# Hash bits for half of the next batch's head pairs, moved from the matrix engine to GpSimd and VectorE

## The chip, the cores and the metric

The kernel runs on one core of one Trainium2 chip. The metric is the device time of one execution in microseconds (us). Engines are named as in the profile: PE is the matrix engine (TensorE) and PEld its weight loads, DVE is VectorE, ACT is ScalarE, POOL is GpSimd, and SP is the engine whose queue issues most of the DMAs. An engine works through its own instructions in the order in which the program lists them; it runs ahead of the other engines as far as its waits allow.

## What is computed

The reference is a hash-masked attention followed by a gated feed-forward block with a residual, in 4 batches of 8 heads, 768 tokens and a head size of 64:

```
bits    = (q @ proj > 0), (k @ proj > 0)            # proj: 64 x 6
mask    = bucket(q)[:, None] == bucket(k)[None, :]  # equal in all six bits
attn    = softmax(where(mask, q @ k.T / 8, -1e9));  x = attn @ v
ffn     = (gelu(x @ w_gate) * (x @ w_val)) @ w_out  # 512 -> 1536 -> 512
out     = x + sigmoid(x @ w_res) * ffn              # 3072 tokens x 512
```

The six bits of each token become +-0.5 values behind the 64 channels of q or k (the tile `nat`). One matmul over 71 rows then gives score and mask penalty together, and `exp` does the rest.

## The kernel before, in words

**Tiling.** Heads go in pairs `p` = 0 to 15, four pairs to a batch. A pair's q (side 0) and k (side 1) are loaded as `[128, 12, 64]` fp32 tiles (`raw`, line 107). `cast` (lines 208, 210, on POOL) writes them as bf16 into `nat`, of which there are four buffers; pair p+2 uses the buffers of pair p. `bits` (line 282) writes the six hash values beside them, and `turn` (line 308) transposes `nat` into `aug` by a DMA from SP. Thus `cast` and `bits` of a pair must wait until the transposing DMA of the pair two before it has landed.

**Stages.** After the first batch's attention (slots 0 to 35, an order written out by hand) the program alternates. A *gate stage* for batch b, `gate_val`, runs 12 steps `m`: 16 matmuls with `w_gate` and 16 with `w_val` into two PSUM buffers `sp` (line 472), a Gelu on ACT (line 489), and the product `hh` on DVE (line 492), which frees the buffer for the next step's second half. Then an *attention stage* for batch b+1 runs 36 slots, nine to a pair: scores (line 448), `exp` on ACT (line 459), the product with v two slots later (line 421), and among these the matmuls of the output projection of batch b (lines 504 and 518), of which DVE makes an output row (lines 521 and 524). Per head, DVE also clears an accumulator (`opened`, line 388), repeats a preset over it (`repeat`, line 400, after the matmul of line 396) and normalises it (`finish`, lines 372 and 373).

**Order around the change.** `gv(b, m, ...)` appends a piece of work behind step m of gate stage b, `at(s, ...)` behind slot s. These set only the order in each engine's queue. For b = 1 and 2 the next batch's first two pairs (`xs`) and last two (`ys`) are prepared so. `tr` (line 240) transposes a raw tile on DVE in 32 x 32 blocks. `hash_mm` (line 251) multiplies these by `proj` on PE, 16 fp32 matmuls in two passes each for two pairs. `hash_tok` (line 266) transposes the sums back, and `bits` takes the signs in four instructions of 32 partitions. In the first attention stage the result of `hash_tok`, `ht`, is in SBUF; later it is in PSUM. `vals_s` and `vals_a` (lines 338 to 350, POOL) prepare v. For `ys`: `tr` at two late slots and behind m = 3 and 5, `cast` behind 5 and 6, `hash_mm` behind 6, `hash_tok` behind 7, `bits` and `turn` behind 7 to 10.

**Last row.** The very last output row is made in two parts, of 384 and 128 columns, each with its matmuls, two DVE instructions and DMA.

Of the kernel before, what the change touches and what calls it, by code (L numbers as in the profile page):

```python
# [9 lines left out]
FP32 = mybir.dt.float32  # L10
BF16 = mybir.dt.bfloat16
AF = mybir.ActivationFunctionType
ALU = mybir.AluOpType
# [33 lines left out]
def kernel(  # L47
# [23 lines left out]
    HT = 2 * T  # L71
# [10 lines left out]
    const = ctx.enter_context(tc.tile_pool(name="const", bufs=1))  # L82
# [19 lines left out]
    x_tok, x_sb = {}, {}  # L102
# [94 lines left out]
    def nat_of(x):  # L197
        return nat[(2 * x[0] + x[1]) % NN]
# [34 lines left out]
    def acc_done(what):  # L233
        accs[len(accs) - 1 - accs[::-1].index(what)] = None

    def tr(p, side, h0=0, h1=2):
        if (p, side) not in t32:
            t32[p, side] = t32_pool.tile([P, HT, 2, 32], FP32, tag="t32", name="t32")
        sl = slice(h0 * T, h1 * T)
        nc.vector.transpose(t32[p, side][:, sl].rearrange("p c h n -> p (c h n)"),  # L240
                            raw[p, side][:, sl].rearrange("p c d -> p (c d)"))
# [15 lines left out]
    def ht_of(jobs):  # L257
        return jobs[0]

    def hash_tok(jobs, psum=False):  # L260
        n = 32 * len(jobs)
        if psum:
            ht = mm_ps.tile([P, HT, 32], FP32, tag=take(("ht", ht_of(jobs))), name="htp")
        else:
            ht = sm_pool.tile([P, HT, 32], FP32, tag="ht", name="ht")
        nc.vector.transpose(ht[:n].rearrange("p c n -> p (c n)"),
                            hsum[jobs[0]][:n].rearrange("p c n -> p (c n)"))
        give(jobs[0])
        for j, x in enumerate(jobs):
            htok[x] = (ht, j)  # L270
        ht_left[id(ht)] = (len(jobs), ("ht", ht_of(jobs)))

    def bits(p, side, engs=(nc.vector,)):
        x = (p, side)
        ht, j = htok.pop(x)
        n, what = ht_left.pop(id(ht))
        if n > 1:
            ht_left[id(ht)] = (n - 1, what)
        else:
            give(what)  # L280
        for a in range(4):
            engs[a % len(engs)].tensor_scalar(  # L282
                nat_of(x)[32 * a:32 * a + 32, :, D:D + NBITS],
                ht[32 * j:32 * j + 32, :, NBITS * a:NBITS * (a + 1)], 0.0, 0.5,
                op0=ALU.is_gt, op1=ALU.subtract)


# [9 lines left out]
    def bits_one(p, side, hi):  # L297
        hs = hsum.pop((p, side, hi))
        nc.vector.transpose(hs[:, 1].rearrange("p c n -> p (c n)"),
                            hs[:, 0].rearrange("p c n -> p (c n)"))  # L300
        nc.vector.tensor_scalar(nat_of((p, side))[:, hi * T:hi * T + T, D:D + NBITS],
                                hs[:, 1, :, 0:NBITS], 0.0, 0.5, op0=ALU.is_gt, op1=ALU.subtract)
        acc_done(("hs", p, side, hi))

    def turn(p, side):
# [29 lines left out]
    def vals_a(p):  # L335
        vs = rawv[p]
        va = va_pool.tile([P, 2, T, D + 2], BF16, tag="va", name="va")
        nc.gpsimd.tensor_copy(va[:, :, :, 0:D], vs)
        nc.gpsimd.memset(va[:, :, :, D:D + 1], 1.0)
        vaug[p] = va  # L340

    def vals_s(p):
        vs = rawv[p]
        vsum = va_pool.tile([P, 2, D + 2], BF16, tag="vsum", name="vsum")
        v3 = sm_pool.tile([P, 2, 3, D], FP32, tag="v3", name="v3")
        nc.gpsimd.tensor_add(v3, vs[:, :, 0:3, :], vs[:, :, 3:6, :])  # L346
        v1 = sm_pool.tile([P, 2, D], FP32, tag="v1", name="v1")
        nc.gpsimd.tensor_add(v1, v3[:, :, 0, :], v3[:, :, 1, :])
# [149 lines left out]
    def project(b):  # L498
        hh = hidden[b]
        for t in range(T):  # L500
            last = b == B - 1 and t == T - 1
            rps = mm_ps.tile([P, DMODEL], FP32, tag=take(), name="rps")
            for kk in range(KM):
                nc.tensor.matmul(rps, x_sb[b][:, kk, t, :], wr[:, kk, :],  # L504
                                 start=(kk == 0), stop=(kk == KM - 1))
                if kk == KM - 1:
                    th = g_pool.tile([P, DMODEL], FP32, tag="th", name="th")
                    nc.scalar.activation(th, rps, AF.Tanh, scale=0.5)  # L508
                yield
            o = o_pool.tile([P, DMODEL], FP32, tag="o", name="o")  # L510
            for k0, k1 in ((0, 3), (3, 4)) if last else ((0, KM),):
                cs = slice(k0 * P, k1 * P)
                if b < B - 1:
                    fps = mm_ps.tile([P, DMODEL], FP32, tag=take(), name="fps")
                else:
                    fps = sc_ps.tile([P, DMODEL], FP32, tag="sp", name="fps")
                for m in range(KF):
                    nc.tensor.matmul(fps[:, cs], hh[:, m, bass.ts(t, P)], wo[:, m, cs],  # L518
                                     start=(m == 0), stop=(m == KF - 1))
                    yield  # L520
                nc.vector.scalar_tensor_tensor(o[:, cs], th[:, cs], 1.0, fps[:, cs],  # L521
                                               op0=ALU.add, op1=ALU.mult)
                o3 = o[:, cs].rearrange("p (k n) -> p k n", n=P)
                nc.vector.scalar_tensor_tensor(o3, o3, 0.5, x_tok[b][:, k0:k1, t, :],
                                               op0=ALU.mult, op1=ALU.add)
                nc.sync.dma_start(out_t[b, t][:, cs], o[:, cs])

# [35 lines left out]
    def at(s, *pieces):  # L563
        side_work.setdefault(s, []).extend(pieces)
# [4 lines left out]
    def gv(b, m, *pieces):  # L569
        gv_work.setdefault((b, m), []).extend(pieces)  # L570
# [92 lines left out]
    for name in ORDER.split():  # L663
        first.pop(name)()

    def lay(b, m, x):
        gv(b, m, lambda: bits(*x), lambda: turn(*x))

    for b in range(B - 1):
        s0, p0 = b * NSLOT, (b + 1) * HP  # L670
        xs = [(p0 + i, side) for i in range(2) for side in range(2)]
        ys = [(p0 + 2 + i, side) for i in range(2) for side in range(2)]
        if b > 0:
            for j, (x, y) in enumerate(zip(xs, ys)):
                at(s0 + 24 + 2 * j, lambda x=x: tr(*x))
                at(s0 + 25 + 2 * j, lambda x=x: cast(*x, nc.gpsimd))
                if j < 2:
                    at(s0 + 32 + 2 * j, lambda y=y: tr(*y))
                loads(s0 + 2 + 4 * j, (x[0], "qk"[x[1]]))
                loads(s0 + 18 + 3 * j, (y[0], "qk"[y[1]]))  # L680
            gv(b, 0, lambda p0=p0: tokens((p0, p0 + 1), True))
            for m, x in zip((0, 1, 2, 4), xs):
                lay(b, m, x)
            gv(b, 3, lambda y=ys[2]: tr(*y))
            gv(b, 5, lambda y=ys[3]: tr(*y))
            for m, y in zip((5, 5, 6, 6), ys):
                gv(b, m, lambda y=y: cast(*y, nc.gpsimd))
            gv(b, 6, lambda p0=p0: hashed((p0 + 2, p0 + 3)))
            gv(b, 7, lambda p0=p0: tokens((p0 + 2, p0 + 3), True))
            for m, y in zip((7, 8, 9, 10), ys):  # L690
                lay(b, m, y)
        else:
            for m, names in enumerate(BESIDE):
                for name in names.split():
                    gv(b, m, first.pop(name))
    for p in range(HP, NPAIR):
# [8 lines left out]
    def mlp_mm(n):  # L705
        while mlp and n > 0:
            try:
# [3 lines left out]
            except StopIteration:  # L711
                mlp.pop(0)

    gate_val(0, begun)
    mlp.append(project(0))
    for s in range(NSLOT, LAST):
# [60 lines left out]
```

## Time and profile before

| | |
|---|---|
| time, median of 3 runs (lowest, highest) | 346.66 us (346.12, 347.13) |
| profiled execution: time, span | 346.07 us, 344.4 us |
| granted PE clock | 0.998 |
| PE busy | 333.5 us, 97% of the span |
| ACT, DVE, POOL busy | 206.2, 191.7 and 85.6 us |
| gate stage of batch 1, of batch 2 | about 129.8 to 162.5 us, 209.5 to 242 us |
| attention of batch 2, of batch 3 | about 162.5 to 209.5 us, 242 to 289 us |

A timeline line has the start and the length in us, the engine, the source line, the operation with its output and inputs, how often it was merged, and in brackets the idle time before it with what ended it. A line of the groups has source line, engine, operation, shapes and count, then busy us and mean ns of one, then idle time before. The span excludes about 1.7 us that lie around it.

### The profile page before, as it was taken

The page shows a single profiled execution, that of the slowest core. Times are in us where ns is not written, and L with a number is a line of the kernel's source. Part 1 is how long each engine was busy: PE and PEld are TensorE (multiplying, and loading weights), DVE is VectorE, ACT ScalarE, POOL GpSimd, SP SyncE. Part 2 cuts the span into 40 slices and gives each one's busy share as a digit, 9 for nine tenths or more (in the row PEclk, how much of TensorE's full clock was granted, in tenths as well). Part 3 has the DMA queues.
Part 4 walks back from the last instruction along what each step waited for, and adds up shares of the span by engine and source line. Part 5 has one row for each costly group of instructions (what it writes and reads, how often), then busy time and mean ns, then how long its engine had stood idle before and what let it go on. Part 6 is the DMA issues. An engine that isn't in the chain of part 4 may idle for free.

```text
span 344.4 us, 7546 instructions
## 1 busy us (share of the span) xinstructions
PE 333.5 (97%) x3064; PEld 204.3 (59%) x3112; DVE 191.7 (56%) x404; ACT 206.2 (60%) x232; POOL 85.6 (25%) x162
## 2 busy tenths in 40 slices
PE   8998999999999999999999999999999999999994
PEld 4675766555666655655666665656566665566442
DVE  6979737656344856757344784747244444343333
ACT  3888972226999962224999982223999984223110
POOL 3887920317055000260043200242030000000000
PEclk9999999999999999999999999999999999999999
DMA  7959998999976743528366642725430220000022
GB/s 215 376 128 280 146 241 149 181 127 176 189 175 188 210 107 78 101 39 148 82 194 188 227 115 65 131 49 109 75 100 32 55 55 30 33 0 0 32 79 75
DMA packets 71171, 42.90 MB, mean 125 GB/s; under 512 B 49504, under 2 KB 68192, under 8 KB 71136
## 3 DMA queue, kind: packets, MB, share of 16 engines
q1 hardware_dynamic: 64720, 37.17, 44.0%
q0 software_dynamic: 6336, 5.24, 10.2%
q8 instruction: 24, 0.39, 0.5%
q14 instruction: 11, 0.09, 0.1%
q10 hardware_dynamic: 80, 0.00, 0.0%
HBM read 29.36 MB, written 6.29 MB: 104 GB/s over the span
## 4 chain that ended last, share of the span: by engine, by line
PE 90%; DVE 3%; ACT 3%; issue 1%; DMA 1%; SPq 0%; POOL 0%; DVEq 0%; ACTq 0%; POOLq 0%
PE sp L472 34%; PE fps L518 18%; PE sp L448 17%; PE av L421 9%; PE rps L504 6%; PE hs L251 3%; ACT hh L459 2%; DMA ld<-in_k_dram 1%; PE pt L320 1%; PE wps L174 1%; DVE nat L282 1%; PE hs L293 1%; DVE aug L329 1%; ACT gt L489 0%; SPq L308 0%
## 5 line engine op out<-in xcount | busy, mean ns | idle before, releaser
L459 ACT ACTIVATE e<-sp 128x1024 bf16<-128x1024 f32 x108 | 109.0, 1028 | 8.0 <-PE sp L448 2.8
L489 ACT ACTIVATE gt<-sp 128x768 bf16<-128x768 f32 x48 | 38.9, 810 | 92.8 <-PE sp L472 92.8
L448 PE MATMUL sp<-aug,aug 71*128 71x256 bf16 (+1 forms) x384 | 85.8, 325 | 2.0 <-DVE aug L329 1.6
L518 PE MATMUL fps<-wo,hh 128*128 128x512 bf16 (+2 forms) x275 | 74.6, 369 | 1.4
L492 DVE TENSOR_TENSOR hh<-gt,sp 128x768 bf16<-128x768 bf16 x48 | 45.7, 953 | 48.0 <-PE sp L472 43.9
L472 PE MATMUL sp<-x_sb,wv 128*128 128x256 bf16 (+1 forms) x378 | 70.6, 325 | 0.7 <-DVE hh L492 0.4
L472 PE MATMUL sp<-x_sb,wg 128*128 128x256 bf16 (+1 forms) x373 | 70.4, 324 | 0.7
L421 PEld LDWEIGHTS <-e 128*128 128x128 bf16 x864 | 40.2, 97 | 25.1
L472 PEld LDWEIGHTS <-wv 128*128 128x128 bf16 x384 | 37.6, 98 | 25.3 <-issue 0.6
L472 PEld LDWEIGHTS <-wg 128*128 128x128 bf16 x384 | 36.7, 98 | 26.0 <-issue 2.3
L421 PE MATMUL av<-va,e 128*128 128x65 bf16 x864 | 43.4, 193 | 0.0
L518 PEld LDWEIGHTS <-hh 128*128 128x128 bf16 x300 | 27.4, 97 | 22.5
L459 ACT ACTIVATE hh<-sp 128x1024 bf16<-128x1024 f32 x36 | 34.4, 1026 | 5.1 <-PE sp L448 5.0
L521 DVE SCALAR_TENSOR_TENSOR o<-th,fps 128x512 f32<-128x512 f32 (+2 forms) x25 | 16.7, 666 | 36.9 <-PE fps L518 30.0
L448 PEld LDWEIGHTS <-aug 71*128 71x128 bf16 x384 | 29.2, 97 | 13.0 <-issue 2.0
L346 POOL TENSOR_TENSOR v<-ldv 128x384 f32<-128x384 f32 x16 | 16.0, 999 | 64.1 <-DMA ldv<-in_v_dram 64.0
L240 DVE STREAM_TRANSPOSE t<-ld 128x768 f32<-128x768 f32 (+1 forms) x34 | 30.5, 912 | 1.6 <-DMA ld<-in_k_dram 1.4
L400 DVE COPY av<-av 128x390 f32<-128x390 f32 x24 | 13.6, 567 | 29.7 <-PE av L396 29.7
L208 POOL TENSOR_SCALAR nat<-ld 128x768 bf16<-128x768 f32 (+1 forms) x16 | 13.8, 860 | 60.1 <-DMA aug<-nat 55.4
L504 PE MATMUL rps<-wr,x_sb 128*128 128x512 bf16 x90 | 25.6, 378 | 0.3
L508 ACT ACTIVATE th<-rps 128x512 f32<-128x512 f32 x24 | 14.3, 594 | 18.5 <-PE rps L504 18.5
L210 POOL CAST nat<-ld 128x768 bf16<-128x768 f32 (+1 forms) x17 | 13.3, 783 | 39.7 <-DMA aug<-nat 38.8
(64 smaller groups left out, 242.5 us busy)
## 6 DMA issues: line engine op xcount, KB each, us to landing
ldv<-in_v_dram SPq DMA_DIRECT2D x16, 384.0 KB, 5.4
out_dram<-o SPq DMA_DIRECT2D x23, 256.0 KB, 2.0
ld<-in_q_dram SPq DMA_DIRECT2D x15, 384.0 KB, 5.6
ld<-in_k_dram SPq DMA_DIRECT2D x15, 384.0 KB, 5.2
wg<-in_moe_w_gate_dram POOLq DMA_DIRECT2D x4, 384.0 KB, 8.5
wv<-in_moe_w_val_dram POOLq DMA_DIRECT2D x4, 384.0 KB, 9.0
wo<-in_moe_w_out_dram POOLq DMA_DIRECT2D x3, 512.0 KB, 9.4
wr<-in_moe_w_res_dram POOLq DMA_DIRECT2D x1, 512.0 KB, 7.7
```

Source lines behind the costliest of these rows:

```text
L240: nc.vector.transpose(t32[p, side][:, sl].rearrange("p c h n -> p (c h n)"), raw[p, side][:, sl].rearrange("p c d -> p (c d)"))
L346: nc.gpsimd.tensor_add(v3, vs[:, :, 0:3, :], vs[:, :, 3:6, :])
L421: nc.tensor.matmul(av[p, hi][:, qt, :], e[:, off:off + P], va[:, hi, jt, 0:D + 1], start=first, stop=(p >= HP and jt == T - 1), skip_group ...
L448: nc.tensor.matmul(sp[:, off:off + nq * P], ks[0:KA, hi * T + jt, :], qs[0:KA, hi * T + qt0:hi * T + qt0 + nq, :], start=True, stop=True)
L459: nc.scalar.activation(e, sp, AF.Exp, scale=float(ALPHA))
L472: nc.tensor.matmul(sp[:, c0:c1], w[:, kk, bass.ts(m, P)], xs[:, kk, c0:c1], start=(kk == 0), stop=(kk == KM - 1))
L489: nc.scalar.activation(gt, sp[:, 0:S], AF.Gelu)
L492: nc.vector.tensor_mul(hidden[b][:, m, :], gt, ps[1][:, 0:S])
L504: nc.tensor.matmul(rps, x_sb[b][:, kk, t, :], wr[:, kk, :], start=(kk == 0), stop=(kk == KM - 1))
L508: nc.scalar.activation(th, rps, AF.Tanh, scale=0.5)
L518: nc.tensor.matmul(fps[:, cs], hh[:, m, bass.ts(t, P)], wo[:, m, cs], start=(m == 0), stop=(m == KF - 1))
L521: nc.vector.scalar_tensor_tensor(o[:, cs], th[:, cs], 1.0, fps[:, cs], op0=ALU.add, op1=ALU.mult)
```

## The change

For b = 1 and 2 the bits of `ys` no longer use PE. `proj` is read once as a row on all partitions and turned to six rows `prow` of 64 (one DMA, one POOL copy, in the first gate stage). For each of the four tiles in `ys` and each of the six bits, POOL multiplies the raw tile by the row (`part`, 768 elements per partition, into a buffer of the ring `t32` of six), DVE sums each run of 64 (`part_sum`), and after six of these one DVE instruction takes the signs (`bits_sum`) and `turn` follows. The lists PROD and SUMS place the 24 products and sums: numbers below 12 stand behind that gate step, 12 and more behind slot n - 12 of the following attention. The `tr`, `hash_mm`, `hash_tok` and `bits` of `ys` are gone. `bits` and `turn` of `xs` move to steps 0, 0, 3, 5, the casts of `ys` to 2, 5, 10, 11, and `vals_s` and `vals_a` to nine and six slots ahead of their pair (both eight before).

Besides: the SBUF result of `hash_tok` gets 15 rows in place of 12, four used and one left out, three times; the first DVE instruction of an output row writes its product over the PSUM input and the second reads it there; the last row is made in parts of 256, 128 and 128 columns, the last of them in another PSUM pool.

```diff
+    def stripes(ht):
+        n = ht.shape[1]
+        return ht.rearrange("p (a c) n -> p a c n", a=3)[:, :, 0:HT // 3] if n > HT else \
+            ht.rearrange("p (a c) n -> p a c n", a=3)
...
-            ht = sm_pool.tile([P, HT, 32], FP32, tag="ht", name="ht")
+            ht = sm_pool.tile([P, HT + 3, 32], FP32, tag="ht", name="ht")
...
-                nat_of(x)[32 * a:32 * a + 32, :, D:D + NBITS],
-                ht[32 * j:32 * j + 32, :, NBITS * a:NBITS * (a + 1)], 0.0, 0.5,
+                nat_of(x)[32 * a:32 * a + 32, :, D:D + NBITS].rearrange("p (a c) n -> p a c n", a=3),
+                stripes(ht[32 * j:32 * j + 32, :, NBITS * a:NBITS * (a + 1)]), 0.0, 0.5,
...
+    hsum6 = const.tile([P, HT + 3, NBITS], FP32, name="hsum6")
+    prow = const.tile([P, NBITS, D], FP32, name="prow")
...
+    def part(x, j):
+        pd = t32_pool.tile([P, HT, D], FP32, tag="t32", name="pd")
+        nc.gpsimd.tensor_mul(pd, raw[x], prow[:, j].unsqueeze(1).to_broadcast([P, HT, D]))
+        hparts[x, j] = pd
+
+    def part_sum(x, j):
+        nc.vector.tensor_reduce(stripes(hsum6)[:, :, :, j],
+                                hparts.pop((x, j)).rearrange("p (a c) d -> p a c d", a=3), axis=mybir.AxisListType.X, op=ALU.add)
+
+    def bits_sum(x):
+        nc.vector.tensor_scalar(nat_of(x)[:, :, D:D + NBITS].rearrange("p (a c) n -> p a c n", a=3),
+                                stripes(hsum6), 0.0, 0.5,
+                                op0=ALU.is_gt, op1=ALU.subtract)
...
-            for k0, k1 in ((0, 3), (3, 4)) if last else ((0, KM),):
+            for k0, k1 in ((0, 2), (2, 3), (3, 4)) if last else ((0, KM),):
...
-                if b < B - 1:
+                if last and k1 == KM:
+                    fps = av_ps.tile([P, DMODEL], FP32, tag="av", name="fps")
+                elif b < B - 1:
...
-                nc.vector.scalar_tensor_tensor(o[:, cs], th[:, cs], 1.0, fps[:, cs],
+                nc.vector.scalar_tensor_tensor(fps[:, cs], th[:, cs], 1.0, fps[:, cs],
...
-                nc.vector.scalar_tensor_tensor(o3, o3, 0.5, x_tok[b][:, k0:k1, t, :],
+                g3 = fps[:, cs].rearrange("p (k n) -> p k n", n=P)
+                nc.vector.scalar_tensor_tensor(o3, g3, 0.5, x_tok[b][:, k0:k1, t, :],
...
+    FROM = 1
+    PROD = (0, 0, 0, 0, 0, 1, 2, 2, 6, 7, 8, 8, 10, 10, 10, 12, 13, 13, 13, 19, 19, 20, 22, 27)
+    SUMS = (1, 2, 2, 4, 5, 6, 7, 8, 9, 10, 10, 11, 12, 12, 13, 17, 19, 21, 21, 23, 23, 29, 30, 31)
+    CASTS = (2, 5, 10, 11)
+    VALS = (9, 6)
+    LAYS = (0, 0, 3, 5)
...
-                if j < 2:
-                    at(s0 + 32 + 2 * j, lambda y=y: tr(*y))
...
-            gv(b, 3, lambda y=ys[2]: tr(*y))
-            gv(b, 5, lambda y=ys[3]: tr(*y))
-            for m, y in zip((5, 5, 6, 6), ys):
+            for m, y in zip(CASTS, ys):
                 gv(b, m, lambda y=y: cast(*y, nc.gpsimd))
-            gv(b, 6, lambda p0=p0: hashed((p0 + 2, p0 + 3)))
-            gv(b, 7, lambda p0=p0: tokens((p0 + 2, p0 + 3), True))
-            for m, y in zip((7, 8, 9, 10), ys):
-                lay(b, m, y)
...
+            for i, (y, j) in enumerate((y, j) for y in ys for j in range(NBITS)):
+                plan.append((PROD[i] + .3, lambda y=y, j=j: part(y, j)))
+                plan.append((SUMS[i] + .2, lambda y=y, j=j: part_sum(y, j)))
+                if j == NBITS - 1:
+                    plan.append((SUMS[i] + .2, lambda y=y: (bits_sum(y), turn(*y))))
+            for n, piece in sorted(plan, key=lambda e: e[0]):
+                put(int(n), piece)
...
-            at(9 * p - 8, lambda p=p: vals_s(p), lambda p=p: vals_a(p))
+            at(9 * p - VALS[0], lambda p=p: vals_s(p))
+            at(9 * p - VALS[1], lambda p=p: vals_a(p))
...
+    gv(0, 9, lambda: pn.append(rows()))
+    gv(0, 11, lambda: rows_turned(pn[0]))
```

More of the change, by code (lines that the diff above doesn't have):

```diff
@@ L264, in hash_tok @@
         else:
-            ht = sm_pool.tile([P, HT, 32], FP32, tag="ht", name="ht")
-        nc.vector.transpose(ht[:n].rearrange("p c n -> p (c n)"),
-                            hsum[jobs[0]][:n].rearrange("p c n -> p (c n)"))
+            ht = sm_pool.tile([P, HT + 3, 32], FP32, tag="ht", name="ht")
+        nc.vector.transpose(stripes(ht[:n]).rearrange("p a c n -> p a (c n)"),
+                            hsum[jobs[0]][:n].rearrange("p (a c) n -> p a (c n)", a=3))
         give(jobs[0])
@@ L303, in bits_one, with rows, rows_turned @@
         acc_done(("hs", p, side, hi))
+    hsum6 = const.tile([P, HT + 3, NBITS], FP32, name="hsum6")
+    prow = const.tile([P, NBITS, D], FP32, name="prow")
+    hparts = {}
+    def rows():
+        pn = o_pool.tile([P, DMODEL], FP32, tag="o", name="pn")[:, 0:D * NBITS]
+        nc.sync.dma_start(pn, proj.rearrange("d n -> (d n)").unsqueeze(0).to_broadcast([P, D * NBITS]))
+        return pn
+    def rows_turned(pn):
+        nc.gpsimd.tensor_copy(prow, pn.rearrange("p (d n) -> p n d", n=NBITS))
+    def part(x, j):
[9 more added lines that the diff above has]
+                                op0=ALU.is_gt, op1=ALU.subtract)
     def turn(p, side):
@@ L681 @@
             gv(b, 0, lambda p0=p0: tokens((p0, p0 + 1), True))
-            for m, x in zip((0, 1, 2, 4), xs):
+            for m, x in zip(LAYS, xs):
                 lay(b, m, x)
-            gv(b, 3, lambda y=ys[2]: tr(*y))
-            gv(b, 5, lambda y=ys[3]: tr(*y))
-            for m, y in zip((5, 5, 6, 6), ys):
+            for m, y in zip(CASTS, ys):
                 gv(b, m, lambda y=y: cast(*y, nc.gpsimd))
-            gv(b, 6, lambda p0=p0: hashed((p0 + 2, p0 + 3)))
-            gv(b, 7, lambda p0=p0: tokens((p0 + 2, p0 + 3), True))
-            for m, y in zip((7, 8, 9, 10), ys):
-                lay(b, m, y)
         else:
@@ L695, with put @@
                     gv(b, m, first.pop(name))
+        if b >= FROM:
+            s1 = s0 + NSLOT
+            def put(n, piece):
+                if n < KF:
+                    gv(b, n, piece)
+                else:
+                    at(s1 + n - KF, piece)
+            plan = []
+            for i, (y, j) in enumerate((y, j) for y in ys for j in range(NBITS)):
[5 more added lines that the diff above has]
+                put(int(n), piece)
     for p in range(HP, NPAIR):
         if p >= HP + 1:
-            at(9 * p - 8, lambda p=p: vals_s(p), lambda p=p: vals_a(p))
+            at(9 * p - VALS[0], lambda p=p: vals_s(p))
+            at(9 * p - VALS[1], lambda p=p: vals_a(p))
         if p >= HP + 3:
@@ L712, in mlp_mm @@
                 mlp.pop(0)
+    pn = []
+    gv(0, 9, lambda: pn.append(rows()))
+    gv(0, 11, lambda: rows_turned(pn[0]))
     gate_val(0, begun)
```

## The prediction

> **What bounds the kernel now.** I read the busy line and the chain's engine shares first, then the stage table (stretch: length, then busy us of each engine, granted clock, DMA).
>
> ```profile
> PE 333.5 (97%) x3064; PEld 204.3 (59%) x3112; DVE 191.7 (56%) x404; ACT 206.2 (60%) x232; POOL 85.6 (25%) x162
> PE 90%; DVE 3%; ACT 3%; issue 1%; DMA 1%; SPq 0%; POOL 0%; DVEq 0%; ACTq 0%; POOLq 0%
> 129.80:162.50 32.70, 32.49 (x244) 19.52 (x246) 21.94 (x50) 10.30 (x13) 8.77 (x16) 1.00 0.48 93
> 162.50:209.50 47.00, 46.45 (x490) 28.61 (x499) 24.57 (x49) 40.78 (x44) 9.35 (x16) 1.00 0.55 155
> ```
>
> PE is the bound in both kinds of stage (32.49 of 32.70 us, 46.45 of 47.00), at full clock, and 90% of the chain. So PE work taken out shortens the span, unless a later DVE or POOL instruction makes PE wait. POOL is nearly empty, DVE about half full.
>
> **1. The hash matmuls: -3.08 us.** The Gelu of each gate step starts when PE has finished that step's first half, so it is the step's clock.
>
> ```profile
> 146.55 0.81 ACT L489 ACTIVATE gt<-sp 128x768 bf16<-128x768 f32 x1 [1.79 <-PE sp L472]
> 147.74 1.51 PE L251 MATMUL hs<-t,projw 128*32 128x192 f32 x32
> 150.69 0.81 ACT L489 ACTIVATE gt<-sp 128x768 bf16<-128x768 f32 x1 [3.33 <-PE sp L472]
> 153.29 0.81 ACT L489 ACTIVATE gt<-sp 128x768 bf16<-128x768 f32 x1 [1.79 <-PE sp L472]
> 226.30 0.81 ACT L489 ACTIVATE gt<-sp 128x768 bf16<-128x768 f32 x1 [1.79 <-PE sp L472]
> 230.44 0.81 ACT L489 ACTIVATE gt<-sp 128x768 bf16<-128x768 f32 x1 [3.33 <-PE sp L472]
> ```
>
> A step takes 153.29 - 150.69 = 2.60 us; the step holding the 32 hash passes takes 4.14, in both batches. Each set therefore costs 1.54, two sets 3.08. ACT waits through both, so nothing else fills that time.
>
> **2. DVE in the gate stages: +0.4.** Per step PE needs 2.60 us, and `hh` must end before the next second half starts.
>
> ```profile
> 140.12 0.95 DVE L492 TENSOR_TENSOR hh<-gt,sp 128x768 bf16<-128x768 bf16 x1 [0.66 <-PE sp L472]
> 140.99 0.97 DVE L240 STREAM_TRANSPOSE t<-ld 128x768 f32<-128x768 f32 x1
> 141.15 1.46 PE L472 MATMUL sp<-x_sb,wv 128*128 128x512 bf16 x8
> 142.72 0.95 DVE L492 TENSOR_TENSOR hh<-gt,sp 128x768 bf16<-128x768 bf16 x1 [0.76 <-PE sp L472]
> 143.70 0.98 DVE L282 TENSOR_SCALAR nat<-htp 32x72 bf16<-32x72 f32 x4
> 33.27 1.84 DVE L240 STREAM_TRANSPOSE t<-ld 128x768 f32<-128x768 f32 x2
> 132.31 0.59 DVE L266 STREAM_TRANSPOSE htp<-hs 128x384 f32<-128x384 f32 x1
> 132.94 0.93 DVE L282 TENSOR_SCALAR nat<-htp 32x72 bf16<-32x72 f32 x4
> 134.92 0.95 DVE L492 TENSOR_TENSOR hh<-gt,sp 128x768 bf16<-128x768 bf16 x1 [1.05 <-PE sp L472]
> ```
>
> `hh` ends at 141.07 and PE goes on at 141.15: 0.08 us to spare. A late `hh` is a stall. No sum stands in this trace. The nearest rows read as many elements: `hh` and the transpose, 0.95 to 0.97, and behind one another they step by 0.87 to 0.88 (140.12 to 140.99; two transposes in 1.84). I take 0.88. Low end: that PE is not held at all. High end: each of a sum's twelve groups as dear as an instruction of its own, the accumulator memset below (0.11), 12 x 0.11 = 1.34.
>
> At 0.88: step 0 has `hh`, one transpose and now eight sign instructions: 132.94 + 2 x 0.93 ends at 134.80, just ahead of 134.92. Steps 2 and 10 hold `hh` and two sums, 0.87 + 2 x 0.88 = 2.63, inside the slack. Step 5 holds `hh`, four sign instructions and a sum: 0.98 + 0.95 + 0.88 = 2.81, 0.21 late, of which 0.13 reaches PE. The other steps hold at most 2.1. With rounding at steps 0, 2 and 10 I put 0.2 a stage, 0.4 together.
>
> **3. POOL: 0.** A product has two inputs of 768 elements.
>
> ```profile
> L346 POOL TENSOR_TENSOR v<-ldv 128x384 f32<-128x384 f32 x16 | 16.0, 999 | 64.1 <-DMA ldv<-in_v_dram 64.0
> L348 POOL TENSOR_TENSOR v<-v 128x128 f32<-128x128 f32 x16 | 7.3, 454 | 1.3
> ```
>
> 256 elements more cost 0.545 us, so 768 cost 0.999 + 384 x 0.00213 = 1.82 (low end 1.0, the row as it is; high end 2.0, the row twice). 24 of them are 44 us in a cycle of some 80 us. The first two run early, in idle POOL. From the third on, the six-buffer ring holds POOL until the `xs` hash has read its tiles, before 132.31 in this batch. From there POOL's queue holds 22 products (40.0), the four casts of `ys` and the v work of two pairs; these last make up all that POOL does in the attention row of the stage table, 9.35. So it is through at 181.7. By the rows of the next part a slot takes 1.12 us (168.58 in slot 5, 178.64 in slot 14), and the last sum, behind slot 19, falls due at 184.3 at the earliest. That is 2.6 to spare over 22 products: up to 1.94 each no sum waits, and the sums before it have more room for each product. Queued behind products are also the casts, which had waited for the transposing DMA anyway, and the v of the batch's second pair, ready at about 169 and wanted at slot 11, 175.3.
>
> The transposing DMA of the last `ys` tile now leaves at slot 19 and is wanted at slot 27, nine microseconds later. SP waits there on `bits_sum` with loads and output DMAs behind it, at most 1 us late; the loads are for the next gate stage and the outputs for nobody.
>
> ```profile
> aug<-nat SPq DMA_TRANSPOSE x24, 3.7
> ```
>
> It lands 3.7 after its issue: covered.
>
> **4. DVE in attention: +0.2.** Twelve sums and two sign instructions per batch fall in slots 0 to 19.
>
> ```profile
> 168.58 0.57 DVE L400 COPY av<-av 128x390 f32<-128x390 f32 x1 [5.04 <-PE av L396]
> 171.30 0.19 DVE L372 RECIPROCAL rec<-av 128x6 f32<-128x6 f32 x1
> 175.07 0.20 DVE L372 RECIPROCAL rec<-av 128x6 f32<-128x6 f32 x1 [1.22 <-PE av L421]
> 175.94 0.11 DVE L388 MEMSET av<- 128x65 f32 x1
> 178.22 0.69 DVE L521 SCALAR_TENSOR_TENSOR o<-th,fps 128x512 f32<-128x512 f32 x1 [2.16 <-ACT e L459]
> 178.64 0.20 PE L396 MATMUL av<-vsum,eps_sb 128*128 128x65 bf16 x1
> 178.94 0.92 DVE L524 SCALAR_TENSOR_TENSOR o<-o,x_tok 128x512 f32<-128x512 f32 x1
> 170.69 0.69 DVE L524 SCALAR_TENSOR_TENSOR o<-o,x_tok 128x512 f32<-128x512 f32 x1
> ```
>
> Slots 0 and 1 are free (5.04 idle). From 168.58 on, in queue order on the old clock: copy, sum, the output row up to 171.30; finish (0.87, as from 175.07 to 175.94) and memset to 172.3; a sum to 173.2; the next copy to 173.85; sum, signs (0.25), sum to 175.9; the finish of 175.07, so 0.8 late, to 176.7; two sums to 178.5; then the memset that stood at 175.94, ending at 178.6. PE's preset at 178.64 needs it: just level. Behind it come the output row and a copy, 0.1 late. I put 0.1 per batch (low end 0, high end the 2.5 of rival A). The remaining three sums meet gaps of 1 to 2 us such as those quoted.
>
> **5. Gaps in the hash result: -1.1.** The same sign instruction reads SBUF in the first attention and PSUM later (min/median/max ns).
>
> ```profile
> L282 DVE TENSOR_SCALAR nat<-htp x96: 214/228/239, 53.3 to 241.3; 32x72 bf16<-32x72 f32 x96
> L282 DVE TENSOR_SCALAR nat<-ht x18: 185/194/1061, 15.6 to 31.1; 32x72 bf16<-32x72 f32 x18
> 29.98 2.21 DVE L282 TENSOR_SCALAR nat<-ht 32x72 bf16<-32x72 f32 x4
> 31.10 1.02 POOL L346 TENSOR_TENSOR v<-ldv 128x384 f32<-128x384 f32 x1
> 33.30 0.39 PE L448 MATMUL sp<-aug,aug 71*128 71x512 bf16 x1 [1.20 <-DVE aug L329]
> 33.78 13.16 ACT L459 ACTIVATE hh<-sp 128x1024 bf16<-128x1024 f32 x14 [1.37 <-PE sp L448]
> ```
>
> The SBUF form is quicker (194 against 228) but is blocked up to 1061 while POOL works. Four of them took 2.21 in place of 0.8, and the copies to `aug` behind them left PE idle for 1.20 and ACT for 1.37. If the gapped form behaves like the PSUM form, that idle time goes, less a tenth for the slower form; if not, nothing goes. Ends 0 and -1.2. I take -1.1: the blocking is tied to the quick form, and the edit alters exactly its access pattern. Behind 33.78 ACT runs 14 exponentials without idle time and PE is as full, so what starts earlier there stays earlier; the loads of the first gate stage stand in SP's queue behind that stage's own transposing DMAs and move with it. The Trainium skill's page "SBUF — State Buffer", section "Who interferes with whom", says that a DVE instruction in a two-port mode and a POOL instruction lock each other out for their whole length; "Advanced Engine Details and Errata", section "VectorE Performance Modes", ties that mode to both outermost counts being even, or odd and equal. By these pages three source runs against twelve destination rows leave the mode.
>
> **6. Rest: -0.35.** The gated row in PSUM: 0. The first instruction, with a PSUM input, takes 0.69 and the second, from SBUF alone, 0.69 too, so a PSUM operand is not dearer; the 0.92 at 178.94 fell beside POOL work. The PSUM bank is free 0.7 later, but its next user, the output matmuls of the following row, comes some seven slots on. Moving `vals`, and the row DMA and copy in the first gate stage (POOL idle there): 0. Last row:
>
> ```profile
> 337.14 2.78 PE L518 MATMUL fps<-wo,hh 128*128 128x384 bf16 x24
> 339.93 0.56 DVE L524 SCALAR_TENSOR_TENSOR o<-o,x_tok 128x384 f32<-128x384 f32 x1
> 340.41 0.28 DVE L521 SCALAR_TENSOR_TENSOR o<-th,fps 128x128 f32<-128x128 f32 x1
> 340.72 0.29 DVE L524 SCALAR_TENSOR_TENSOR o<-o,x_tok 128x128 f32<-128x128 f32 x1
> ```
>
> PE ends at 339.92, yet the last pair starts at 340.41 behind the 384-column pair. With 256 columns first, PE ends that part at about 338.6 (two thirds of the 384 columns' share); its pair, 0.42 each (halfway between 0.28 and 0.56), is done by 339.5; the middle pair ends at 340.1, so the last starts behind PE at 340.0 to 340.1 and ends at 340.65 instead of 341.01. The third output DMA is small and SP issues it in the time of the others.
>
> **Sum.** 346.07 - 3.08 + 0.4 + 0.2 - 1.1 - 0.35 = 342.1 for the profiled execution. The median of the runs lies 0.59 higher, so I predict 342.7.
>
> **Rivals.** *A, dear sums (slower).* If sums step by more than 0.88, each further 0.1 costs a gate stage about 0.2 + 0.2 + 0.1 (steps 2, 10 and 5) and an attention 0.6 (six sums ahead of the memset), 2.2 over both batches. Above 1.06 a sum the gain of 3.9 is gone; at 1.34 the time is 342.7 + 4.6 x 2.2 = 352.8. Against it: two kinds of 768-element rows agree on 0.88. Chance 0.10 above 1.06, and 0.15 for 0.95 to 1.06, which ends between 344.2 and 346.6. The Trainium skill's page "VectorE: DVE Perf Modes", section "Rules for kernel authors", speaks for this rival: it calls `tensor_reduce` the slowest DVE operation and says to expect its plain mode; no run here shows one yet.
> *B, POOL late (slower).* Above 1.94 a product the sums of slots 11 to 19 wait for POOL, and `repeat` and `finish` behind them. At 2.3 they are 22 x 0.36 = 7.9 late, some 6 of it on PE, twice: 355. Against it: two rows of other sizes put the product at 1.82. Chance 0.05.
> *C, the gaps change nothing (the change does not do what it says there).* The sign instructions of the first attention stay open to blocking, PE waits 1.2 us at 33 as before: 342.7 + 1.1 = 343.8. For it: the edit leaves output, sizes and engine alone. Against it: the PSUM form shows that the instruction has a form that POOL does not touch. Chance 0.12.
>
> **How the numbers follow.** Forecast 0.58, with its own range of 341.6 (no stall in parts 2 and 4, and the full 1.2 of part 5) to 343.4. Faster by over 0.3% (1.04 us, about what a measurement of this kernel can tell from no change): the forecast, C and most of the mild half of A, 0.83; same, the rest of that half, 0.04; slower 0.13. The range takes in C and most of the mild A, 341.6 to 345.8, and leaves out the dear end.
>
> **What would show it.** Right: all gate steps of batches 1 and 2 but step 0 at 2.60 to 2.8; sums of 0.95; products of 1.8; no DVE sign instruction over 0.25 us before 35 us, and no PE wait at 33; the last DVE pair right behind PE's end. Wrong: PE waiting for `hh` in most steps, or for the memset in attention; DVE waiting for a product.

## The result

The changed kernel takes 341.37 us (median of 4 runs, 341.02 to 342.38) beside 346.45 us for the kernel before on the same chip: ratio 0.9856, 95% interval 0.9829 to 0.9883. A second comparison in the course of the experiments gave 342.02 beside 346.46 us, 0.9871 (0.9853 to 0.9888). The two differences are 5.1 and 4.4 us; 3.9 was forecast. The direction was right and the size too small: the first median lies 0.2 us below the predicted range, the second inside it. By stages, the mechanisms of parts 1 to 5 came as forecast; what was missed most lies at the very end, behind the last DVE instruction.

The page of the changed kernel, its busy line and the chain's shares:

```profile
PE 331.5 (97%) x3012; PEld 204.2 (60%) x3060; DVE 217.6 (64%) x420; ACT 206.3 (61%) x232; POOL 170.1 (50%) x211
PE 87%; ACT 4%; DVE 3%; DMA 2%; issue 2%; SPq 1%; POOL 0%; DVEq 0%
```

POOL has twice its old load and DVE 26 us more, and PE is still busy for 97% of a span that is shorter. The new work, by groups (line, engine, operation, shapes, count, then busy us and mean ns of one, then idle time before):

```profile
L324 POOL TENSOR_TENSOR pd<-ld,prow 128x768 f32<-128x768 f32 x48 | 86.2, 1815 | 38.5 <-PE hs L251 34.4 <-DVE hsum L328 4.0
L328 DVE TENSOR_REDUCE hsum<-pd 128x12 f32<-128x768 f32 x48 | 44.4, 943 | 0.5
```

A product takes 1.815 us (1.82 was worked out), a sum 0.943 (0.95). Products waited 4.0 us in all for a sum to free a buffer of the ring, while DVE stood idle for only 0.5 us ahead of its sums: the sums did not wait for POOL.

**The opening is chance.** The profiled execution of the changed kernel is the slowest of its four, and a stretch ahead of anything that was changed explains it: the two profiled executions of this kernel, 342.38 and 341.04 us, differ by as much as their first scores (8.77 and 7.43). The first eight hash matmuls and the first scores, in three profiles (before, after, and the changed kernel again, label e5_after):

```profile
4.24 1.93 PE L293 MATMUL hs<-t,projs 128*128 128x192 f32 x8
```

```profile
4.24 2.84 PE L298 MATMUL hs<-t,projs 128*128 128x192 f32 x8
8.77 0.60 PE L479 MATMUL sp<-aug,aug 71*128 71x512 bf16 x2 [0.38 <-DVE aug L360]
```

```profile
4.24 1.50 PE L298 MATMUL hs<-t,projs 128*128 128x192 f32 x8
7.43 0.61 PE L479 MATMUL sp<-aug,aug 71*128 71x512 bf16 x2 [0.38 <-DVE aug L360]
```

They start at 4.24 us everywhere and take 1.50 to 2.84, so the first scores start between 7.43 and 8.77 (7.86 in the profile of before). Compared from the first scores on, the span went from 344.4 - 7.86 = 336.54 to 340.7 - 8.77 = 331.93, and to 331.87 in the second profile: 4.6 to 4.7 us less. The table splits all profiles at the Gelus of the gate stages: first scores, from there to the first Gelu, first to last Gelu of the gate stages of batches 1 and 2, the attention stages between, and from the last Gelu of all to the end.

| kernel | first scores | to first Gelu | gate 1, gate 2 | attention of batches 1, 2, 3 | end |
|---|---|---|---|---|---|
| before | 7.86 | 42.99 | 30.71, 30.71 | 49.04, 49.04, 48.71 | 26.49 |
| after | 8.77 | 41.63 | 29.53, 29.53 | 49.04, 49.04, 48.71 | 25.57 |
| e5_after, again | 7.43 | 41.62 | 29.54, 29.53 | 49.03, 49.04, 48.71 | 25.51 |
| e1_gaps | 7.55 | 41.62 | 30.71, 30.71 | 49.30, 49.04, 48.71 | 26.45 |
| e2_tail3 | 7.44 | 43.09 | 30.71, 30.71 | 49.05, 49.04, 48.70 | 25.91 |
| e3_psum | 8.68 | 43.02 | 30.72, 30.71 | 49.04, 49.04, 48.70 | 26.46 |
| e4_hash | 7.92 | 42.61 | 29.53, 29.53 | 49.09, 49.42, 48.81 | 26.32 |
| e6_step4 | 8.16 | 41.62 | 29.16, 29.17 | 49.05, 49.05, 48.70 | 25.59 |
| e7_nopsum | 8.69 | 41.61 | 29.53, 29.53 | 49.31, 49.43, 48.81 | 25.48 |
| e8_sum2att | 8.38 | 41.63 | 29.53, 29.53 | 49.04, 57.70, 58.49 | 25.51 |
| e9_onedma | 8.49 | 41.62 | 29.53, 29.53 | 49.04, 49.04, 48.70 | 26.01 |
| e10_prod | 7.70 | 41.62 | 29.53, 29.53 | 49.04, 49.04, 48.70 | 25.60 |

So the change is -1.36 ahead of the first Gelu, -1.18 in each of two gate stages, 0 in attention and -0.92 at the end, 4.64 in all, with 0.03 given back in the first gate stage. (The span is given to 0.1 us, so a figure of the last column is good to 0.05.)

**Gate stages.** The Gelus around the step that is still long, and the instructions of DVE and PE that lead to it:

```profile
146.13 0.81 ACT L520 ACTIVATE gt<-sp 128x768 bf16<-128x768 f32 x1 [1.79 <-PE sp L503]
148.73 0.81 ACT L520 ACTIVATE gt<-sp 128x768 bf16<-128x768 f32 x1 [1.79 <-PE sp L503]
151.69 0.81 ACT L520 ACTIVATE gt<-sp 128x768 bf16<-128x768 f32 x1 [2.15 <-PE sp L503]
154.29 0.81 ACT L520 ACTIVATE gt<-sp 128x768 bf16<-128x768 f32 x1 [1.79 <-PE sp L503]
```

```profile
142.30 0.95 DVE L523 TENSOR_TENSOR hh<-gt,sp 128x768 bf16<-128x768 bf16 x1 [0.66 <-PE sp L503]
143.17 0.95 DVE L328 TENSOR_REDUCE hsum<-pd 128x12 f32<-128x768 f32 x1
144.90 0.95 DVE L523 TENSOR_TENSOR hh<-gt,sp 128x768 bf16<-128x768 bf16 x1 [0.78 <-PE sp L503]
145.89 0.99 DVE L287 TENSOR_SCALAR nat<-htp 32x72 bf16<-32x72 f32 x4
146.90 0.95 DVE L328 TENSOR_REDUCE hsum<-pd 128x12 f32<-128x768 f32 x1
147.89 0.95 DVE L523 TENSOR_TENSOR hh<-gt,sp 128x768 bf16<-128x768 bf16 x1
148.90 1.46 PE L503 MATMUL sp<-x_sb,wv 128*128 128x512 bf16 x8 [0.20 <-DVE hh L523]
```

The step of 4.14 us is gone, as forecast, and one of 2.96 stands in its place. It follows gate step 5, with `hh`, four sign instructions and a sum, as forecast too, but dearer: the next `hh` starts 147.89 - 144.90 = 2.99 after its forerunner, 0.39 late, and the long step carries 0.36, so this step lies outside the 2.60 to 2.8 that the prediction gave as its sign. The sum steps by 0.99 there; after a sum elsewhere `hh` follows in 0.86 to 0.87. By the Trainium skill's page "VectorE: DVE Perf Modes", section "Two Vector instructions with no wait between them", an instruction is held until all earlier ones have finished where its operands start in another group of 32 partitions than those before. The trace agrees: the full length is paid on each side of the sign instructions, which work on 32 partitions at a time (142.30 to 143.17 is 0.87, 144.90 to 145.89 is 0.99).

### The profile page after: what moved, and what is told of

Same layout as the page of the kernel before. It is cut to its first block, busy times and chain, and to the rows that moved or that the text cites. A ratio compares the mean times of both kernels' runs of the same rounds, so it can differ in the third digit from the quotient of the medians.

```text
span 340.7 us, 7546 instructions
## 1 busy us (share of the span) xinstructions
PE 331.5 (97%) x3012; PEld 204.2 (60%) x3060; DVE 217.6 (64%) x420; ACT 206.3 (61%) x232; POOL 170.1 (50%) x211
## 2 busy tenths in 40 slices
DMA packets 71459, 43.09 MB, mean 126 GB/s; under 512 B 49536, under 2 KB 68480, under 8 KB 71424
## 4 chain that ended last, share of the span: by engine, by line
PE 87%; ACT 4%; DVE 3%; DMA 2%; issue 2%; SPq 1%; POOL 0%; DVEq 0%
PE sp L503 32%; PE fps L551 17%; PE sp L479 17%; PE av L452 9%; PE rps L535 6%; ACT hh L490 3%; PE hs L251 2%; DVE hh L523 1%; DMA ld<-in_q_dram 1%; DMA ld<-in_k_dram 1%; PE pt L351 1%; DVE nat L287 1%; SPq L125 0%; ACT gt L520 0%; PE hs L298 0%
## 5 line engine op out<-in xcount | busy, mean ns | idle before, releaser
L324 POOL TENSOR_TENSOR pd<-ld,prow 128x768 f32<-128x768 f32 x48 | 86.2, 1815 | 38.5 <-PE hs L251 34.4
L503 PE MATMUL sp<-x_sb,wg 128*128 128x512 bf16 (+1 forms) x375 | 70.5, 325 | 0.6
L328 DVE TENSOR_REDUCE hsum<-pd 128x12 f32<-128x768 f32 x48 | 44.4, 943 | 0.5
L551 PEld LDWEIGHTS <-hh 128*128 128x128 bf16 x312 | 28.1, 97 | 21.8
L554 DVE SCALAR_TENSOR_TENSOR fps<-th,fps 128x512 f32<-128x512 f32 (+2 forms) x26 | 16.9, 650 | 28.1 <-PE fps L551 26.7
L240 DVE STREAM_TRANSPOSE t<-ld 128x768 f32<-128x768 f32 (+1 forms) x26 | 22.8, 895 | 1.6 <-DMA ld<-in_k_dram 1.4
```

The lines of the kernel that those rows point to most:

```text
L324: nc.gpsimd.tensor_mul(pd, raw[x], prow[:, j].unsqueeze(1).to_broadcast([P, HT, D]))
L328: nc.vector.tensor_reduce(stripes(hsum6)[:, :, :, j], hparts.pop((x, j)).rearrange("p (a c) d -> p a c d", a=3), axis=mybir.AxisListType.X ...
L503: nc.tensor.matmul(sp[:, c0:c1], w[:, kk, bass.ts(m, P)], xs[:, kk, c0:c1], start=(kk == 0), stop=(kk == KM - 1))
L554: nc.vector.scalar_tensor_tensor(fps[:, cs], th[:, cs], 1.0, fps[:, cs], op0=ALU.add, op1=ALU.mult)
```

## The experiments

All times are medians beside the kernel before on the same chip and in the same series (346.26 us for the first four, 346.46 for e5 to e8, 346.2 for e9 and e10).

### The gaps alone (e1_gaps)

```diff
-            ht = sm_pool.tile([P, HT, 32], FP32, tag="ht", name="ht")
+            ht = sm_pool.tile([P, HT + 3, 32], FP32, tag="ht", name="ht")
```

with `stripes` in `hash_tok` and `bits` as in the change.

> The kernel before with the gaps in the hash result alone. Theory: all blocking of the sign instructions before 35 us goes (none over 0.25 us), the 1.20 us wait of PE at 33 goes, and since ACT, idle there for 1.37, sets the pace behind it, the gain is 1.37 us in span, not 1.1: the first Gelu comes 1.4 earlier counted from the first scores. Rival (no effect of gaps; the gain came from POOL work falling otherwise): sign instructions up to 1 us, same time as before.

Measured: 344.88 us, ratio 0.9963 (0.9948 to 0.9977). The first Gelu comes 41.62 us behind the first scores, 1.37 earlier than before. The sign instructions of the first attention, first as one line of their source (min/median/max ns), then the four that had taken 2.21 us:

```profile
L287 DVE TENSOR_SCALAR nat<-ht x18: 215/219/225, 15.3 to 29.9; 32x72 bf16<-32x72 f32 x18
29.23 0.91 DVE L287 TENSOR_SCALAR nat<-ht 32x72 bf16<-32x72 f32 x4
```

None is over 0.225 us, and each costs 25 ns more than the quick form did. The PE wait of 1.20 is gone. The theory holds, and the size is that of ACT's idle time: behind it ACT, not PE, sets the pace. One thing was not expected: batch 1's attention is 0.26 longer (49.30), which the change as a whole does not show. e7 comes back to it.

### The last row in three parts alone (e2_tail3)

```diff
-            for k0, k1 in ((0, 3), (3, 4)) if last else ((0, KM),):
+            for k0, k1 in ((0, 2), (2, 3), (3, 4)) if last else ((0, KM),):
```

with the last part in the other PSUM pool.

> The kernel before with the last row in three parts alone (the gated row stays in SBUF). Theory: the last VectorE pair starts right behind PE, 0.35 us earlier, and the end follows it by 2.8 in place of 3.4 us, since the transfer ahead of the last one is 64 KB in place of 192 KB: 0.9 us in all. Rival (only the instruction order counts, the rest of the profiled difference was chance): 0.35 us, and 3.4 us from the last VectorE instruction to the end.

Measured: 345.3 us, ratio 0.9975 (0.996 to 0.999). In the profile the last Gelu is at 317.69 and the last DVE instruction here:

```profile
span 343.6 us, 7622 instructions
339.81 0.28 DVE L523 SCALAR_TENSOR_TENSOR o<-th,fps 128x128 f32<-128x128 f32 x1
340.13 0.29 DVE L526 SCALAR_TENSOR_TENSOR o<-o,x_tok 128x128 f32<-128x128 f32 x1
```

It ends 22.73 behind the last Gelu, 23.10 before: -0.37, as forecast. The end follows 3.18 later; before it was 3.39. In this profile the gain behind the last instruction is thus only 0.2, and neither theory's figure was met: between the two. The medians, 0.96 apart, are nearer to the theory, but the interval reaches down to 0.35. The 3.18 also speaks against the theory's reason, for the transfer ahead of the last one is 64 KB here; e9 comes back to it.

### The gated row in PSUM alone (e3_psum)

```diff
-                nc.vector.scalar_tensor_tensor(o[:, cs], th[:, cs], 1.0, fps[:, cs],
+                nc.vector.scalar_tensor_tensor(fps[:, cs], th[:, cs], 1.0, fps[:, cs],
```

and the second instruction reads `fps`.

> The kernel before with the gated row in PSUM alone. Theory: no difference within 0.1 us; second instruction of an output row at 0.69 in all 23 rows, where 0.89 and 0.92 stood. Rival (the second instruction's collisions with POOL cost time on the path): 0.3 us or more faster.

Measured: 346.46 us, ratio 1.0 (0.9986 to 1.0013), all stages as before. The second instruction never takes over 0.692. Alone this part is worth nothing that shows.

### The hash move alone (e4_hash)

The changed kernel without the three other parts (the diffs above taken back).

> The change without gaps, without three parts and with the gated row in SBUF: the hash move alone. Theory: -3.08 for the matmuls and +0.36 at one gate step of each of batches 1 and 2, so 2.36 us faster, and the attention of batches 2 and 3 as long as before. Rival (the second instruction of an output row, with two SBUF inputs, now meets POOL products all the time): attention longer by 0.5 us or more, gain under 1.9.

Measured: 344.09 us, ratio 0.9941 (0.9925 to 0.9956), 2.2 us faster. The gate stages give exactly the 2.36. Batch 2's attention is 0.38 longer and batch 3's 0.10, and the second instruction of an output row (two SBUF inputs) is slower:

```profile
L556 DVE SCALAR_TENSOR_TENSOR o<-o,x_tok 128x512 f32<-128x512 f32 x23 | 18.6, 807 | 0.8
```

0.807 us in the mean, up to 1.35, in place of 0.715. The rival's mechanism exists, at 0.5 us in place of more. The four sign instructions, here without the gaps, still take 2.21 us, so it is the gaps that end their blocking. The first Gelu comes 0.38 earlier than before all the same: the POOL product of v with which they collide starts that much earlier, counted from the first scores (30.78 - 7.92 against 31.10 - 7.86). With the gaps this is worth nothing more (41.63 in after, 41.62 in e1).

### The changed kernel again (e5_after)

> The changed kernel once more, beside the next three. Theory: hash -2.36, gaps -1.37, last row -0.35 by its last VectorE instruction and up to -0.5 by a shorter output transfer behind it: 4.1 to 4.6 us faster than before, once the opening (first scores at 7.4 to 8.8 us, by chance) is the same; attention of batches 2 and 3 as long as before (49.0 us from the last Gelu of one gate stage to the first of the next). Rival (parts help one another): over 4.8 us.

Measured: 342.02 us, ratio 0.9871 (0.9853 to 0.9888), and from the first scores to the end 331.87 us, 4.67 less than before. That is just above the theory's upper end and below the rival's 4.8; the theory's reason for up to 0.5 of it, a shorter transfer, does not hold (e9).

### One sum moved by a step (e6_step4)

```diff
-    SUMS = (1, 2, 2, 4, 5, 6,
+    SUMS = (1, 2, 2, 4, 4, 6,
```

> The changed kernel with one sum moved from behind gate step 5 to step 4, so that no step holds hh, four sign instructions and a sum. Theory: the one long step (2.96 us) of each of batches 1 and 2 goes back to 2.60, 0.72 us faster than the changed kernel. Rival (two sums at step 4 are as bad, or the product is not there yet): the long step moves to step 5 or 6, no gain.

Measured: 341.07 us, ratio 0.9848 (0.9832 to 0.9864), 0.95 below the changed kernel in the same series, of which the stages show 0.74: the two gate stages are 0.37 shorter each, and every distance between two Gelus but the first (3.17) is 2.60. With 29.16 against 30.71 the whole 1.54 of a hash set is now gained. Step 4 now carries two sums (142.58) and the next `hh` is not late:

```profile
141.71 0.95 DVE L523 TENSOR_TENSOR hh<-gt,sp 128x768 bf16<-128x768 bf16 x1 [0.66 <-PE sp L503]
142.58 1.81 DVE L328 TENSOR_REDUCE hsum<-pd 128x12 f32<-128x768 f32 x2
144.31 0.95 DVE L523 TENSOR_TENSOR hh<-gt,sp 128x768 bf16<-128x768 bf16 x1
```

It is the quickest version of all.

### The change with the gated row in SBUF (e7_nopsum)

The diff of e3 taken back, the rest as changed.

> The changed kernel with the gated row in SBUF as before. Theory: the second instruction of an output row, with two SBUF inputs, is blocked by POOL products (up to 1.35 us in place of 0.69) and batch 2's attention grows by 0.38 as it did in the hash move alone, so 0.4 us slower than the changed kernel; POOL products up to 0.7 us longer where they wait. Rival (that 0.38 was another wait): attention as in the changed kernel.

Measured: 342.5 us, ratio 0.9891 (0.9875 to 0.9908), 0.5 above the changed kernel. Attention grows by 0.27, 0.39 and 0.10 in the three batches: the excess of e1 in batch 1 and of e4 in batches 2 and 3. One place where the two engines meet:

```profile
177.88 0.94 DVE L558 SCALAR_TENSOR_TENSOR o<-o,x_tok 128x512 f32<-128x512 f32 x1
178.26 2.22 POOL L324 TENSOR_TENSOR pd<-ld,prow 128x768 f32<-128x768 f32 x1
```

DVE takes 0.94 in place of 0.69 and the product 2.22 in place of 1.81. So the gated row in PSUM, worth nothing in the old kernel, keeps the other parts' gains whole: some 0.75 us over three attentions by the stages.

### Dearer sums in attention (e8_sum2att)

```diff
-    def part_sum(x, j):
+    def part_sum(x, j, again=False):
+        if again:
+            nc.vector.tensor_reduce(stripes(hsum7)[:, :, :, j],
+                                    hparts[x, j].rearrange("p (a c) d -> p a c d", a=3), axis=mybir.AxisListType.X, op=ALU.add)
```

with `again` for the sums behind slots.

> The changed kernel with every sum in attention done twice (the second result unused), 0.88 us more for each of 12 sums a batch. By rival A's price (all of the six sums ahead of the memset reach PE): 5.1 us a batch, 10 us slower than the changed kernel. Rival reading (VectorE has slack of a microsecond or more between these slots): under 6 us.

Measured: 360.89 us, ratio 1.0414 (1.039 to 1.0439): 18.9 us above the changed kernel. Rival A's place was right, and the cost is nearly twice what its price gave. PE waits for the accumulator memset, and for the very one that part 4 of the prediction named:

```profile
167.91 0.19 PE L431 MATMUL av<-vsum,eps_sb 128*128 128x65 bf16 x1 [1.37 <-DVE av L423]
182.78 0.19 PE L431 MATMUL av<-vsum,eps_sb 128*128 128x65 bf16 x1 [4.12 <-DVE av L423]
```

But DVE's lateness behind the three sums of slots 0 and 1 reaches PE as well, once they are doubled (the 1.37), and so does that behind the three later ones (0.73 at 195.82). Of the 12 x 0.88 = 10.6 us added to DVE in a batch, PE waited 6.2 for the memset in each of the two attentions. The attentions grew by more, 8.7 and 9.8, because PE was slower behind the long wait. The next two lines have the stretch, its length, the busy us of PE, PEld, DVE, ACT and POOL, then the granted clock and two columns on DMA:

```profile
184.00:186.00 2.00, 2.00 (x13) 1.01 (x12) 0.57 (x2) 1.11 (x2) 1.93 (x4) 0.50 0.63 156
270.00:275.00 5.00, 4.99 (x28) 2.56 (x28) 2.64 (x7) 1.51 (x2) 1.56 (x5) 0.50 0.14 52
```

The granted clock is 0.66 in the mean of 183 to 188 us and 0.52 from 270 to 276, where it is 1.00 in the changed kernel; by these figures 5 x 0.34 = 1.7 and 6 x 0.48 = 2.9 us were lost (an estimate), most of the 2.4 and 3.6 that the waits leave over. The changed kernel's attention stands close under a DVE bound.

### The output of the last row in larger pieces (e9_onedma)

```diff
-                nc.sync.dma_start(out_t[b, t][:, cs], o[:, cs])
+                if last and k0 == 0:
+                    continue
+                ds = slice(0, k1 * P) if last and k0 == 2 else cs
+                nc.sync.dma_start(out_t[b, t][:, ds], o[:, ds])
```

> The changed kernel with the output of the last row's first two parts sent by one DMA of 192 KB behind the second part, as much as the kernel before sends ahead of its last part. Theory: the last VectorE instruction ends as in the changed kernel, and the end follows it by about 3.4 us in place of 2.8, for the last transfer lands behind a larger one: 0.5 us slower than the changed kernel. Rival (the shorter end comes from elsewhere): 2.8 as in the changed kernel.

Measured: 341.96 us; the ratio, 0.9882 (0.9862 to 0.9903), cannot tell half a microsecond, but the profile can. The last DVE instruction ends at 337.75 and the span at 341.0: 3.25 us, near the theory's 3.4. With three transfers it is 2.82 in the profile of after, 2.76 in e5 and 2.75 in e7; with the old two 3.39, 3.35 (e1), 3.33 (e3) and 3.22 (e4); e2, with three, has 3.18. The theory's reason is wrong, though: the last transfer does not land later behind a larger one. Its issue, and the time from there to its landing (min/median/max of this one transfer), before, after and here:

```profile
341.04 0.33 SPq L526 DMA_DIRECT2D out_dram<-o  x1
DMA to landing us min/median/max: 1.6/1.6/1.6
```

```profile
337.91 0.33 SPq L560 DMA_DIRECT2D out_dram<-o  x1
DMA to landing us min/median/max: 1.5/1.5/1.5
```

```profile
337.78 0.33 SPq L563 DMA_DIRECT2D out_dram<-o  x1
DMA to landing us min/median/max: 1.6/1.6/1.6
```

In all twelve profiles the last transfer lands 1.54 to 1.59 us behind the last DVE instruction. What differs is the time from this landing to the end of the span: 1.76 before, 1.22 after, 1.63 here. Over the twelve profiles it takes three values, and they go with the number of DMAs that SP issues in the whole program: 1.73 to 1.76 with 112 (before, e1, e3), 1.62 or 1.63 with 113 (e2, e4, e9), 1.22 to 1.24 with 114 (after, e5, e6, e7, e8, e10). The change adds two, the row of `proj` and the third output part. At its end SP works through a list of waits for its DMAs; behind the last landing the first two groups have one pause of 0.35 to 0.37 us between two of these waits, the third has none. e9 issues one DMA fewer than the changed kernel, so it changed the count together with the bytes; e2, which by its bytes should go with the changed kernel, goes by its count with e4 and e9. But no run changes the count alone, and why the pause goes stays open.

### Dearer products (e10_prod)

```diff
         hparts[x, j] = pd
+        nc.gpsimd.tensor_copy(nopool[:, 0:NCOPY], prow.rearrange('p n d -> p (n d)')[:, 0:NCOPY])
```

> The changed kernel with a small POOL copy (128 elements, some 0.3 us, result unused) behind each of the 48 products, so that a product costs POOL about 2.1 us in place of 1.78. By the prediction's bound of 1.94, 22 products are 3.5 late at the last sum, 2 to 3 of that on PE in each of batches 2 and 3: 4 to 6 us slower than the changed kernel, gate stages as before. Rival (POOL has more room than the bound says): under 1 us slower.

Measured: 341.91 us, ratio 0.9882 (0.986 to 0.9904), all stages as in the changed kernel. The rival reading was right. With the copy a product steps by 2.00, not 2.1, and the last one of batch 2 is through just as its sum falls due:

```profile
181.56 1.81 POOL L326 TENSOR_TENSOR pd<-ld,prow 128x768 f32<-128x768 f32 x1
183.40 0.95 DVE L331 TENSOR_REDUCE hsum<-pd 128x12 f32<-128x768 f32 x1
```

So 2.00 is still free, and the bound is not at 1.94 but at 2.00 or above; nothing above was tried. POOL's waits for ring buffers (4.0 us in the changed kernel) are gone in this one; the longer step fills them.

## Why the prediction fell short

**Right.** The bound and the sign. Part 1 to the hundredth: the long steps are gone. Part 3: product 1.815 against 1.82, through in time, with 2.00 still free where 1.94 stood as the limit. Part 4's account of DVE in attention: the memset forecast to be just level (178.6) starts at 176.85 on a clock that is 1.6 earlier, and PE does not wait:

```profile
175.04 1.80 DVE L328 TENSOR_REDUCE hsum<-pd 128x12 f32<-128x768 f32 x2
176.85 0.11 DVE L419 MEMSET av<- 128x65 f32 x1
```

Part 5's mechanism, and in part 6 the order of the last DVE instructions behind PE's end:

```profile
334.36 2.81 PE L551 MATMUL fps<-wo,hh 128*128 128x256 bf16 x36
337.27 0.29 DVE L554 SCALAR_TENSOR_TENSOR fps<-th,fps 128x128 f32<-128x128 f32 x1
337.59 0.29 DVE L558 SCALAR_TENSOR_TENSOR o<-fps,x_tok 128x128 f32<-128x128 f32 x1
```

**Mis-sized terms.** The sum was -3.93 and should have been -4.61 on the profile of before.
- Part 6, -0.35 for the last row: -0.92 in after. This is the largest miss and the step that failed. The account stopped at the last DVE instruction, and up to there it was right (23.10 behind the last Gelu before, 22.75 after: -0.35). The time from there to the end was put at nothing without a look: 3.39 before, 2.82 after, another -0.57. "SP issues it in the time of the others" was true and not the point. Nearly all of it (1.76 to 1.22, 0.54) lies behind the landing of the last transfer and goes with the number of DMAs on SP's queue (e9); its cause stays open.
- Part 5, -1.1 for the gaps: -1.37 alone, -1.36 in after. It took PE's idle time (1.20), less a tenth, where ACT's (1.37) was the one on the path; the row with ACT's idle time was quoted there.
- Part 4, +0.2: 0.
- Part 2, +0.4: 0.72. The step was named rightly (5), but it was summed to 2.81 and took 2.99: a sum behind sign instructions was priced at 0.88 where it costs 0.99, and the four sign instructions at 0.95 where they step by 1.01. Of the 0.39 by which `hh` is late 0.36 reaches PE, where 0.13 of 0.21 was forecast.
- Part 6, 0 for the gated row in PSUM: right by itself, but only because of it part 4 is 0. Put in SBUF it costs about 0.5 us in the medians and 0.76 by the stages (e7).

**The step from the profile to the median.** 0.59 us was added, since the median of the runs lay that much above the profiled execution. That is chance rather than a property of the kernel: the opening alone is 1.3 us wide over these profiles, and the median of before in the later series was 346.2 to 346.5. Without it 342.1 would have stood there. With the four terms mended it is 341.5, between the two measured medians. The lower end, 341.6, contained no price for the time behind the last DVE instruction; and by the reasons given for it (no stall in parts 2 and 4, the full 1.2 of part 5) it would have been 342.7 - 0.7 = 342.0.

**Rivals.** C is excluded by e1. A's place was right. Its price of 0.6 per 0.1 us in an attention was near for the waits, 6.2 us for 0.88 more or 0.7, and too low for the whole, 8.7 to 9.8 or 1.0 to 1.1, since the price left out the lower clock behind a long wait. B's limit was slightly low.

## What to carry to other kernels

Where one engine's idle time is to go, take the row of the engine that sets the pace behind it, and follow the last row to the end of the span, past the last compute instruction: 0.57 of the 0.92 us gained at the end lay there, nearly all of it behind the last landing. Price a long wait of the bounding engine by more than its length where the clock falls behind it. A part that measures as nothing alone (the gated row in PSUM) can be what keeps another part's gain whole, so try it inside the whole change too. And subtract what the run owes to chance ahead of the change before two spans are compared.

## What the runs showed of the hardware

- The same eight fp32 matmuls took 1.50 to 2.84 us from the same start at 4.24, with the granted clock given as 1.00 in that stretch. The Trainium skill's page "TensorE: Matmul & The Clock Gate", section "What's actually happening", has the clock rise after a window that runs freely, so the point varies by chance. The spread agrees with that, and so do the single matmuls, with a median of 527 ns in after and 326 in e5_after; the clock column does not show it, and no run here tells the cause apart.
- Behind the 4.12 us for which PE waited in e8, the granted clock was 0.50 (184 to 186 us; 270 to 275 us behind the same wait in the next attention); behind the waits of 1.37 and 0.73 us it stayed at 1.00.
- The last transfer, 64 KB, landed 1.5 to 1.6 us behind its issue in all twelve profiles, whether the one ahead of it had 64 or 192 KB.
- A DVE instruction with two SBUF inputs and a POOL product lengthened each other (0.69 to 0.94, 1.81 to 2.22); with one input in PSUM neither did. A sum, with one SBUF input, took 0.943 in the mean amid products. This is the rule of the Trainium skill's page "SBUF — State Buffer", section "Who interferes with whom", and the traces agree.
- The sign instruction with a gapped source kept clear of POOL at a cost of 25 ns each (219 against 194).
